# Left halo copies of the last chunk issued one feature block ahead on GpSimd

## The chip, the cores and the metric

One core of one Trainium2 chip. The metric is the device time of one execution in microseconds (us); the span that the profile shows is some 3.8 to 4.3 us shorter.

## The reference

A conformer block on x of 2 x 4000 x 512: feed-forward, attention, convolution module, feed-forward. The part concerned is the convolution module:

```python
h = a * sigmoid(b)                                # a, b: the two halves of layernorm(x2) @ w_pw1
hp = pad(h, one row of zeros before and after each sequence)
dc = sum(hp[:, i:i+T, :] * dw[i] for i in range(3))
dc = (dc - mean(dc)) / sqrt(var(dc) + 1e-5)       # per feature, over all 8000 tokens
x3 = x2 + silu(dc) @ w_pw2
```

## The kernel before

Tokens go in 16 chunks of 508 (444 for the last of each sequence), features in four blocks (jj or cc = 0 to 3). Of a chunk's gated values G, each block has one more column on either side, the halo, copied from the neighbour chunk or set to zero. Most of the convolution runs beside attention. For the last chunk (`last` = 15), and for parts of the two before it (`tail` = 14, and 13), it cannot, and stands in the open between attention and the second feed-forward. The mean and variance of a feature need all chunks, so this stretch ends in a dependence of everything on the last block.

The words used below: the taps are the three-tap convolution, here as matmuls on TensorE; the statistics and the aggregate (VectorE) give a feature's mean and variance; the power (GpSimd) and the shift (VectorE) turn them into a scale and an offset; a swish (ScalarE) is the silu of the normalised values. In code and views PE is TensorE, PEld its weight load, DVE VectorE, ACT ScalarE and POOL GpSimd.

The helper `S.op` makes an instruction wait for the last writer of each buffer that it reads or writes, and for the readers of those that it writes, unless an earlier wait of the same engine covers it already. `b_Gl` and `b_Gr` are the halo columns.

```python
def conv_a(self, t, jj):
    ps, b_ps = self.pw1(t, jj)                        # 4 matmuls on TensorE
    out = self.G[gs][:, jj, 1:1 + W]
    wr = [self.b_G[gs][jj], self.b_Gl[gs][jj], self.b_Gr[gs][jj]]
    ...                                               # tail: gates built elsewhere
    elif t == NCK - 1:
        self.halo_left(t, jj)
        self.S.op("DVE", ...scalar_tensor_tensor(     # the gate
            out=out, in0=ps[:, 0:W], scalar=2.0, in1=th, op0=ALU.mult, op1=ALU.mult),
            reads=[b_ps, self.b_th[k]], writes=wr)
    ...
    self.halo_right(t, jj)

def halo_left(self, t, jj):
    ...   # GpSimd: copy of one column from the chunk before, and for the last chunk
    ...   # of a sequence a memset of the right edge column

def conv_scale(self, cc):
    S.op("DVE", ...bn_aggr(...))                      # aggregate
    S.op("POOL", ...tensor_tensor(..., op=ALU.pow))   # power: 1/sqrt(var)

# the main loop over the blocks (cuts marked)
for jj in range(DC):
    self.conv_b(last, jj)                             # 4 matmuls, sigmoid on ACT
    if jj == DC - 1:
        self.act(self.nr1, self.onef, AF.Silu, ...)   # brings the table load here
    copy_away()                                       # ACT: PSUM banks of earlier taps to SBUF
    self.conv_a(last, jj)
    if jj > 1:
        self.conv_shift(jj - 2)                       # DVE: -mean/sqrt(var), reads the power
    if jj:
        finish(jj - 1)                                # taps on TensorE, statistics on DVE, conv_scale
    else:
        ...
self.swish(0, 0); self.swish(0, 1)                    # ACT
copy_away()
...
def between():
    self.conv_shift(DC - 2)
    self.swish(0, 2)
finish(DC - 1, between)                               # between its two statistics
self.conv_shift(DC - 1)
self.swish(0, 3)
copy_away()
```

## Time and profile before

| what | value |
|---|---|
| median, three runs (all that the prediction had) | 2045.01 us (2044.95 to 2045.12) |
| the profiled execution | 2043.9 us, span 2040.1 us |
| TensorE busy | 2029.2 us, 99% |
| two waits of the gate for the halo | 1.86 us in all |
| ACT idle before the last swish of chunk 0 | 0.68 us |

Read it so: TensorE carries nearly the whole span, so only the few places where the chain leaves it are worth anything. The kernel's lines are L1100 (gate), L1206 (statistics), L1213 (aggregate), L1215 (power), L1220 (shift), L1185 and L1188 (left halo and edge memset), L1195 (right halo). All matmuls have line L506 and all ACT instructions L556, those of a helper; "keys" on ACT are the bank copies, "work<-keys" the swishes. The changed kernel's lines are one or two less.

One measure is used below for every kernel. The chain of each trace has a run of 40 matmuls after attention and one of 20 at the second feed-forward. The time from the start of the one to the start of the other is called **the stretch**.

```profile
1516.88 8.74 PE s L506 x40
...
1551.66 4.32 PE s L506 x20
```

In the kernel before it is 1551.66 - 1516.88 = 34.78 us.

### The profile page before, as it was taken

How to read it: one execution, taken by the hardware profiler on the slowest of the kernel's cores; microseconds unless marked ns; L12 is line 12 of the kernel's file. 1: busy time of each engine (PE TensorE's matmuls, PEld its weight loads, DVE VectorE, ACT ScalarE, POOL GpSimd, SP SyncE). 2: the span in 40 equal slices, each digit the busy share in tenths (PEclk: the TensorE clock that was granted, in tenths of full speed). 3: DMA queues.
4: the chain of work that ended last, by engine and by line, in shares of the span. 5: the costliest groups of instructions: out<-in, count | busy, mean ns of one | idle time of the engine just before them, and what ended most of it. 6: DMA issues, size and time to landing. Idle time of an engine off the chain costs nothing.

```text
span 2040.1 us, 24550 instructions
## 1 busy us (share of the span) xinstructions
PE 2029.2 (99%) x9665; PEld 1029.8 (50%) x9667; DVE 1081.1 (53%) x2187; ACT 746.9 (37%) x1280; POOL 107.7 (5%) x235
## 2 busy tenths in 40 slices
PE   9999999999999999999999999999999999999998
PEld 5555555554444444445444444444455555555555
DVE  4234443334556667666766676667674444434433
ACT  3433333333333333333333333333345443443433
POOL 1000000000000000000000000000011000000000
PEclk9999999999999999999999999999999999999999
DMA  8222245320101111114421111111143111111111
GB/s 185 52 62 62 53 100 126 96 70 8 27 16 26 25 33 26 25 25 95 108 57 23 26 28 33 24 26 26 44 135 93 32 31 42 32 31 42 28 35 38
DMA packets 253122, 104.43 MB, mean 51 GB/s; under 512 B 193412, under 2 KB 252487, under 8 KB 252999
## 3 DMA queue, kind: packets, MB, share of 16 engines
q1 hardware_dynamic: 252751, 102.61, 20.9%
q8 instruction: 78, 1.28, 0.3%
q14 instruction: 45, 0.37, 0.1%
q10 hardware_dynamic: 248, 0.18, 0.0%
HBM read 33.77 MB, written 23.34 MB: 28 GB/s over the span
## 4 chain that ended last, share of the span: by engine, by line
PE 98%; DVE 1%; ACT 0%; DMA 0%; SPq 0%; POOL 0%; issue 0%; DVEq 0%; ACTq 0%
PE s L506 56%; PE y L506 42%; ACT work L556 0%; DVE wff L1206 0%; DMA wff<-in_w_ff_a_dram 0%; SPq L568 0%; POOL work L1215 0%; DVE work L553 0%; DVE wff L1100 0%; PE y L534 0%; ACT keys L556 0%; DVE work L1213 0%; SPq L560 0%; DVE work L869 0%; DVE work L952 0%
## 5 line engine op out<-in xcount | busy, mean ns | idle before, releaser
L556 ACT ACTIVATE work<-s 128x508 bf16<-128x508 f32 (+3 forms) x1060 | 622.7, 588 | 1211.8 <-PE s L506 1208.2
L506 PE MATMUL s<-work,wff 128*128 128x508 bf16 (+5 forms) x2624 | 628.3, 371 | 1.5 <-DVE work L553 0.8
L506 PE MATMUL s<-work,keys 128*128 128x508 bf16 (+1 forms) x2048 | 516.7, 374 | 0.1
L506 PE MATMUL y<-work,keys 128*128 128x508 bf16 (+2 forms) x2048 | 504.2, 373 | 0.4 <-DVE work L553 0.4
L506 PE MATMUL y<-wff,work 128*127 128x512 bf16 (+1 forms) x2000 | 501.4, 378 | 0.0
L952 DVE TENSOR_TENSOR work<-work 128x508 f32<-128x508 f32 (+2 forms) x496 | 334.6, 675 | 282.9 <-ACT work L556 281.8
L506 PEld LDWEIGHTS s<-work,wff 128*128 128x128 bf16 x2624 | 252.3, 98 | 278.0 <-issue 5.0
L506 PEld LDWEIGHTS y<-wff,work 128*127 128x127 bf16 x2000 | 274.4, 137 | 170.8
L506 PEld LDWEIGHTS s<-work,keys 128*128 128x128 bf16 x2048 | 199.4, 98 | 231.9 <-issue 0.6
L506 PEld LDWEIGHTS y<-work,keys 128*128 128x128 bf16 (+1 forms) x2048 | 193.5, 97 | 234.0 <-issue 6.2
L755 DVE SCALAR_TENSOR_TENSOR xt<-y,xt 127x512 bf16<-127x512 f32 x125 | 77.8, 684 | 364.9 <-PE y L506 364.9
L618 DVE BATCH_NORM_STATS2 work<-xt 127x6 f32<-127x512 bf16 x311 | 195.5, 678 | 4.8 <-DMA xt<-in_x_dram 4.7
L506 PE MATMUL s<-work 128*127 128x512 bf16 (+3 forms) x776 | 196.2, 377 | 1.6 <-DVE work L1324 1.2
L625 POOL TENSOR_TENSOR work<-work 127x4 f32<-127x4 f32 (+1 forms) x76 | 76.5, 1007 | 1130.4 <-DVE work L623 1130.4
L506 PEld LDWEIGHTS s<-work 128*127 128x127 bf16 (+1 forms) x776 | 94.7, 124 | 75.7 <-issue 2.7
L638 DVE TENSOR_SCALAR work<-xt,work 127x512 bf16<-127x512 bf16 x306 | 110.4, 407 | 27.0 <-POOL work L625 23.2
L755 DVE SCALAR_TENSOR_TENSOR xt<-s,xt 127x512 bf16<-127x512 f32 x55 | 38.0, 692 | 148.6 <-PE s L506 148.6
L755 DVE SCALAR_TENSOR_TENSOR xt<-s,work,xt 127x512 bf16<-127x512 f32 x64 | 48.0, 750 | 30.8 <-PE s L506 30.2
L1104 DVE SCALAR_TENSOR_TENSOR wff<-wff,s 128x508 bf16<-128x508 f32 (+1 forms) x57 | 38.7, 679 | 41.4 <-PE s L506 41.2
L556 ACT ACTIVATE wff<-s 128x508 f32<-128x508 f32 (+1 forms) x67 | 39.5, 591 | 54.6 <-PE s L506 54.6
L556 ACT ACTIVATE work<-keys,work 128x508 bf16<-128x508 bf16 (+1 forms) x68 | 52.3, 775 | 0.8 <-DVE work L1220 0.7
L1185 POOL COPY wff<-wff 128x1 bf16<-128x1 bf16 x56 | 10.4, 187 | 637.8 <-DVE wff L1104 635.0
(92 smaller groups left out, 415.7 us busy)
## 6 DMA issues: line engine op xcount, KB each, us to landing
keys<-keysd SPq DMA_DIRECT2D x62, 128.0 KB, 2.3
keysd<-work SPq DMA_DIRECT2D x14, 448.0 KB, 3.2
out_dram<-work SPq DMA_DIRECT2D x14, 448.0 KB, 3.2
dcvd<-wff SPq DMA_DIRECT2D x48, 127.0 KB, 1.8
keys<-dcvd SPq DMA_DIRECT2D x12, 508.0 KB, 5.4
xt<-in_x_dram SPq DMA_DIRECT2D x13, 448.0 KB, 4.7
wff<-in_w_ff_a_dram SPq DMA_DIRECT2D x16, 256.0 KB, 5.0
work<-work SPq DMA_TRANSPOSE x208, 2.5
```

Of the source, the lines that this page charges most:

```text
L506: self.S.op("PE", lambda e: e.matmul(out, lhsT, rhs, start=start, stop=stop, **kw), reads=reads, writes=[bank], inc=stop if inc is None el ...
L556: return self.S.op("ACT", lambda e: e.activation(out, in_, func, **kw), reads=reads, writes=writes)
L618: self.S.op("DVE", lambda e: e.bn_stats(self.st[sl][:, ti, 0:6], x), reads=[b_x], writes=[self.b_st[sl][ti]])
L625: S.op("POOL", lambda e: e.tensor_tensor(out=self.rs[sl][:, 0:n], in0=self.mv[sl][:, 0:n, 1], in1=self.neghalf[0:TILE, 0:n], op=ALU.pow), ...
L638: self.S.op("DVE", lambda e: e.tensor_scalar(out, x, self.mv[sl][:, ti, 0:1], self.rs[sl][:, ti:ti + 1], ALU.subtract, ALU.mult), reads=[b ...
L755: self.S.op("DVE", lambda e: e.scalar_tensor_tensor(out=self.XT[g][rows], in0=ps[rows], scalar=scalar, in1=self.XT[g][rows], op0=ALU.mult, ...
L952: S.op("DVE", lambda e, p=p, n=n, acc=acc: e.tensor_tensor(out=acc, in0=acc, in1=self.P[p][0:n, 0:W], op=ALU.add), reads=[self.b_P[p], sel ...
L1104: self.S.op("DVE", lambda e: e.scalar_tensor_tensor(out=out, in0=th, scalar=1.0, in1=ps[:, 0:W], op0=ALU.add, op1=ALU.mult), reads=[b_ps, ...
L1185: S.op("POOL", lambda e: e.tensor_copy(self.G[gs][:, jj, 0:1], self.G[gp][:, jj, CHUNK:CHUNK + 1]), reads=[self.b_G[gp][jj]], writes=[self ...
```

## The change

Its intent: the gate of a block should not wait for the batch norm power of a block two before it, only because the power stands ahead of the halo in GpSimd's queue. The left halo needs the chunk before alone, so it can be issued a block earlier.

```diff
@@ conv_a
         elif t == NCK - 1:
-            self.halo_left(t, jj)
             self.S.op("DVE", ...)
@@ main loop
+        self.halo_left(last, 0)
         for jj in range(DC):
             self.conv_b(last, jj)
             ...
             self.conv_a(last, jj)
             if jj > 1:
                 self.conv_shift(jj - 2)
+            if 0 < jj < DC - 1:
+                self.halo_left(last, jj + 1)
             if jj:
                 finish(jj - 1)
             else:
+                self.halo_left(last, 1)
                 f, copy = self.depthwise(tail - 1, DC - 1)
```

## The prediction

> **What bounds the kernel now.** I read the busy times, then the chain that ended last, then the same chain and the engine timelines in the one short stretch that the change touches.
>
> ```profile
> PE 2029.2 (99%) x9665; PEld 1029.8 (50%) x9667; DVE 1081.1 (53%) x2187; ACT 746.9 (37%) x1280; POOL 107.7 (5%) x235
> PE 98%; DVE 1%; ACT 0%; DMA 0%; SPq 0%; POOL 0%; issue 0%; DVEq 0%; ACTq 0%
> ```
>
> TensorE (PE) is busy 99% of the 2040.1 us span and carries 98% of the chain. The other engines together have about 2% of the chain. The change adds, drops and shrinks no instruction: it reorders eight tiny GpSimd (POOL) ones. So it can only move the time where the chain is off PE. The granted clock is 1.000, so there is nothing to win there.
>
> The change acts in the hand-over from attention to the second feed-forward, at 1524 to 1552 us, where the last chunk's four feature blocks (jj = 0 to 3) pass through the gate, the depthwise taps and the batch norm. The chain's pieces there:
>
> ```profile
> 1534.19 0.23 DVE work L1213
> 1534.42 0.07 issue
> 1534.49 0.55 POOL work L1215
> 1535.04 0.14 POOL wff L1185
> 1535.18 0.04 POOL wff L1188
> ...
> 1535.34 0.62 DVE wff L1100
> ...
> 1537.66 0.55 POOL work L1215
> 1538.21 0.14 POOL wff L1185
> 1538.35 0.04 POOL wff L1188
> ...
> 1538.51 0.32 DVE wff L1100
> ```
>
> L1213 is the batch norm aggregate, L1215 its power on GpSimd, L1185 and L1188 the left halo copy and the right edge memset of the next block, L1100 the gate multiply on VectorE (DVE) that writes the same G tile. The gate multiply is declared to write the halo column too, so it waits for the copy and memset; these stand behind the power in GpSimd's queue; the power waits for the aggregate. So the gate of block 2 waits for the norm of block 0, and that of block 3 for block 1: two detours. The waits of this stretch price them:
>
> ```profile
> DVE wff L1100 <- POOL wff L1188: 1.9, 2, 0.9
> ```
>
> Two waits of 0.93 us each. But the chain is not all of it: what follows in the queues decides how much is given back.
>
> ```profile
> 1535.89 1.66 PE L506 MATMUL s<-work,wff 128*128 128x444 bf16 x8
> 1539.38 1.38 PE L506 MATMUL y<-wff 128*128 128x444 bf16 x6 [0.19 <-ACT keys L556]
> 1544.36 1.08 PE L506 MATMUL s<-work 128*127 128x512 bf16 x4 [0.41 <-ACT work L556]
> ```
>
> PE runs without a gap from 1529.83 to about 1539.0; it never stands for the two DVE waits themselves (the table by stretches gives PE 3.10 of 3.10 us and 3.17 of 3.17 in the two block periods). The first gap after them ends on an ACT copy that empties a PSUM bank. The second ends on the last swish of chunk 0, and there the lateness of DVE comes due:
>
> ```profile
> 1537.40 1.28 ACT L556 ACT_TABLE_LOAD   x1
> 1543.50 0.81 ACT L556 ACTIVATE work<-keys,work 128x508 bf16<-128x508 bf16 x1 [0.68 <-DVE work L1220]
> ```
>
> ACT works without a pause from 1537.40, stands idle once for 0.68 us until the last shift (L1220), and is then full again (7.26 of 7.26 us in 1544.40 to 1551.66), through the copies, four swishes of chunk 1 and two layer norm tiles. After 1551.66 PE is again continuous. So **the 0.68 us of ACT idle is what the change can win**, not the 1.86 us of DVE idle.
>
> **What the Trainium skill says.**
> - "Perfetto Trace Analysis", section Tensor Engine Instruction: ACT, DVE and GPSIMD are strict FIFO. The trace agrees: the copy at 1534.99 starts 0.50 us after the power at 1534.49, though its data had been ready since 1525.99.
> - "GPSIMD Engine Reference", section 2.1 Instruction dispatch: completion gates what waits on the semaphore and does not hold back the next Pool instruction. The trace agrees: copies of 0.19 us start 0.12 us apart (1528.61, 1528.72, 1528.84). So the two moved instructions take about 0.23 us of GpSimd per block wherever they stand, not their summed durations.
> - "ScalarE: Activation LUTs", section What ACT_TABLE_LOAD costs: about 1283 ns, plus a drain of about 1380 ns. The trace agrees on the first (1.28 us) and shows no drain: the next ACT instruction starts at 1538.70, 1.30 us after the load started. I use 1.30.
>
> **The change part by part.**
>
> *Blocks 0 and 1: nothing.* Their halo copies move in the source, but GpSimd's order stays as it was: block 0's copy still follows the right halo of the chunk before, block 1's still follows the right halo of block 0. Gates at 1530.83 and 1532.24 unmoved.
>
> *Blocks 2 and 3, GpSimd.* Copy and memset now follow the right halo of the block before (1532.92, and the one after gate 2) and stand before the power. They are done at about 1533.3 for block 2, 1.2 us before that power's aggregate is there. The power itself is not delayed: GpSimd idled 1.38 and 1.45 us before it. Cost 0.
>
> *Gate of block 2.* Without the halo wait it waits for PE only. Gate 1, which did so, started at 1532.24, 0.10 us after its matmuls' modelled end (1530.48 + 1.66 = 1532.14). For block 2: 1533.19 + 1.66 + 0.10 = 1534.95, was 1535.34: 0.39 earlier. DVE is free since 1534.41.
>
> *Gate of block 3.* 1535.89 + 1.66 + 0.10 = 1537.65, was 1538.51: **0.86 earlier**. DVE is free: gate 2 at 1534.95, then 0.54 to the shift, 0.06 to the two statistics of 1.35, aggregate of 0.25, done by 1537.1 or so. PE's pace sets this, not DVE's; of 1.86 us of waits about 0.86 survives here.
>
> *Statistics of block 2.* Gate 3 at 1537.65, shift at 1538.19, statistics to 1539.6, aggregate from 1539.64 (was 1540.50).
>
> *Statistics of block 3.* Here the first give-back: the depthwise matmuls of block 3 cannot start before 1539.38, because their bank is emptied by an ACT copy that stands behind the table load (1537.40 + 1.30 + about 0.1, copy 1538.81 to 1539.3). That doesn't move, as the ACT queue before it hangs on PE. Their first half ends at about 1540.15, the second at 1540.76. So the first statistics go at 1540.2 (was 1540.66) and the second at 1540.86 (was 1541.59): **0.73 earlier**. From there 1.91 us to the last swish, as before (statistics, aggregate, power, shift: 1541.59 to 1543.50): 1542.77.
>
> *ACT.* The swish before it starts at 1542.00, and swishes follow each other about 0.7 us apart (four in 2.90), so ACT is free at about 1542.7. The last swish goes at 1542.77, 0.73 earlier; the idle of 0.68 shrinks to almost nothing. Its third neighbour, PE: the last four matmuls of chunk 0's second pointwise product follow at 1543.7 instead of 1544.36, some 0.62 to 0.66 earlier (PE is busy with the third group of four, loaded at 1542.87, until then).
>
> *After that.* ACT's full stretch moves by about 0.7, DVE's layer norm stretch from 1544.83 by about 0.62, and both meet in the transposes before 1551.66. The smaller shift holds: **0.65 us**, as a middle. The weights for the second feed-forward are loading (DMA share 1.00 and 1.09), but the last are issued at 1543.07 with 7.0 us to landing, and first used at 1555.82; a shift of 0.65 leaves a margin of several us for the first ones.
>
> *Added.* The shifts of blocks 0 and 1 now need a wait on the power of their own (the gate's wait covered it before), already fulfilled: hundredths of a us, in DVE time with slack.
>
> Sum: 2045.01 - 0.65 = **2044.36 us**, 0.03%.
>
> **The rivals.**
> 1. *The full waits come off:* 2 x 0.93 = 1.86 us, 2043.15. For: the chain names these very pieces. Against: PE has no gap in the two block periods, and its 2.70 us per block (1533.19 to 1535.89) is longer than what remains of DVE's 3.17 (3.17 - 0.93 = 2.24). Only the part beyond PE's pace can be won.
> 2. *The bank copies hold everything:* ACT's table load is the true bound, and the last swish has another wait; 2045.0. For: the first PE gap ends on that copy. Against: ACT shows a real idle of 0.68 us before the last swish, and its releaser is the shift on DVE.
> 3. *The gain is hidden by the weights:* the stretch after 1538.5 has a saturated DMA, and PE would then wait for a weight block in the second feed-forward; 2044.7 to 2045.0. For: DMA share 1.09. Against: no DMA wait stands in the chain here now.
> 4. *Slower:* the power delayed behind a halo that waits. The left halos wait for depthwise matmuls of the chunk before last that ended by 1530.5, so I see nothing for it.
>
> **Range and chances.** The main road is worth 0.6 to 0.7; rivals 2 and 3 together have perhaps one chance in six and pull up to 2045.0; rival 1 in part (a further 0.3 from ACT) one in ten. The three runs before differ by 0.17 us. So 2043.8 to 2045.0. Two per cent is 41 us, beyond anything a 28 us stretch can give: within 2% at 0.98.
>
> **What would show it.** Right: in the changed trace GpSimd has copy, memset and then the power twice; the two waits of L1100 on L1188 are gone; gate 3 starts about 0.86 earlier relative to its matmuls; PE's gap before the depthwise matmuls on the ACT copy stays at about 0.19; ACT's idle before the last swish falls from 0.68 to under 0.15; PE's gap of 0.41 before the last four matmuls shrinks to near 0. Wrong: gate 3 early but the last swish not (rival 2); the swish early but a new PE wait on a weight load after 1551 us (rival 3); the block period falling clearly below 2.70 us (rival 1).

## The result and the profile after

| | median us | lowest to highest | runs |
|---|---|---|---|
| before | 2045.07 | 2044.95 to 2045.14 | 4 |
| changed | 2043.54 | 2042.86 to 2044.69 | 4 |

The ratio is 0.9993, 95% interval 0.9976 to 1.001: within 2%, and 1.53 us between the medians, where 0.65 was predicted. The measured median lies below the predicted range (2043.8 to 2045.0).

The stretch in the chain of the changed kernel:

```profile
1517.07 8.74 PE s L506 x40
...
1551.13 4.32 PE s L506 x20
```

It is 34.06 us, 0.72 less than before. Here are the pieces between (cuts marked), which before led four times through the power on GpSimd:

```profile
1536.24 0.77 PE s L506 x4
...
1537.03 0.54 ACT wff L556
...
1537.59 1.28 ACT L556
...
1539.09 0.91 ACT keys L556 x2
1540.00 1.39 ACT work L556 x2
1541.39 0.91 ACT keys L556 x2
1542.30 1.47 ACT work L556 x2
1543.77 0.91 ACT keys L556 x2
1544.68 4.12 ACT work L556 x6
```

From 1530 us on no GpSimd and no DVE piece is left: TensorE hands over to ACT at the gate function of block 3 (1537.03), and from there the view gives everything to ACT: the table load, the copies and the swishes. The order on GpSimd (its timeline; columns: start, duration, engine, line, operation) is the intended one:

```profile
1533.23 0.19 POOL L1184 COPY wff<-wff 128x1 bf16<-128x1 bf16 x1
1533.34 0.10 POOL L1187 MEMSET wff<- 128x1 bf16 x1
1534.67 0.55 POOL L1214 TENSOR_TENSOR work<-work 128x1 f32<-128x1 f32 x1 [1.23 <-DVE work L1212]
```

The gates now wait for their matmuls alone (DVE's timeline; in brackets the idle time before and what ended it):

```profile
1535.13 0.62 DVE L1099 SCALAR_TENSOR_TENSOR wff<-s,wff 128x444 bf16<-128x444 f32 x1 [0.54 <-PE s L506]
...
1537.84 0.62 DVE L1099 SCALAR_TENSOR_TENSOR wff<-s,wff 128x444 bf16<-128x444 f32 x1 [0.47 <-PE s L506]
```

The last two swishes of chunk 0 (ACT's timeline) and the last 16 matmuls of its pointwise product (TensorE's) now follow each other, where before 0.68 and 0.41 us of idle time stood ahead of the last ones:

```profile
1542.18 1.59 ACT L556 ACTIVATE work<-keys,work 128x508 bf16<-128x508 bf16 x2
```

```profile
1541.22 3.77 PE L506 MATMUL s<-work 128*127 128x512 bf16 x16
```

The two views hide a close finish. Asked for the last swish and the last shift alone, ACT's and DVE's timelines give:

```profile
1542.96 0.81 ACT L556 ACTIVATE work<-keys,work 128x508 bf16<-128x508 bf16 x1
```

```profile
1542.77 0.16 DVE L1219 SCALAR_TENSOR_TENSOR work<-work 128x1 f32<-128x1 f32 x1 [0.73 <-POOL work L1214]
```

The last swish starts 0.19 us after the shift, as it did before (1543.30 and 1543.50). In an unbroken pair the second swish follows 0.70 us after the first, so ACT would have been ready at 1542.88. The shift on DVE still comes last, by 0.08 us, and ACT's queue stands right behind it.

So the stretch gave 0.72 us, nearly the predicted 0.65. Where are the other 0.8 us of the medians? The two profiled spans differ by 0.9 (2040.1 and 2039.2), and this can be laid out whole. The chain reaches its 40 matmuls at 1516.88 before and at 1517.07 after: the changed kernel was 0.19 us **behind** before the change had touched anything. The stretch takes 0.72 off. From the 20 matmuls to the issue of the last store on ACT's queue both take the same (1551.66 to 2036.71 is 485.05; 1551.13 to 2036.17 is 485.04). From that issue to the end of the span it is 3.4 us before and 3.0 after. The sum: +0.19 - 0.72 - 0.01 - 0.33 = -0.87. Beside the change the two traces differ in their opening and in the landing of the last store, and nowhere else to a few hundredths of a us.

### The profile page after: what moved, and what is told of

Its sections match the earlier page's. It is cut to its first block, busy times and chain, and to the rows that moved or that the text cites. A ratio compares the mean times of both kernels' runs of the same rounds, so it can differ in the third digit from the quotient of the medians.

```text
span 2039.2 us, 24554 instructions
## 1 busy us (share of the span) xinstructions
PE 2029.2 (100%) x9667; PEld 1030.0 (51%) x9667; DVE 1080.7 (53%) x2187; ACT 746.0 (37%) x1280; POOL 107.6 (5%) x235
## 4 chain that ended last, share of the span: by engine, by line
PE 98%; ACT 1%; DVE 0%; DMA 0%; SPq 0%; issue 0%; ACTq 0%
PE s L506 56%; PE y L506 42%; ACT work L556 0%; DMA wff<-in_w_ff_a_dram 0%; ACT keys L556 0%; SPq L568 0%; DVE work L553 0%; PE y L534 0%; ACT L556 0%; SPq L560 0%; DVE work L869 0%; DVE work L952 0%; DVE wff L1205 0%; DVE wff L1092 0%; ACT wff L556 0%
```

## The experiments

**Theory A**: the change is worth 0.72 us, and the rest is spread from run to run, at the beginning and the end. **Theory B**: the change wins some 0.8 us more somewhere. Within A, further runs ask what the mechanism is: what the halves of the change do, what a longer power costs before and after, and what bounds the stretch now.

The stretch of each kernel, from its chain (start of the 40, start of the 20):

| kernel | 40 | 20 | stretch | against before |
|---|---|---|---|---|
| before | 1516.88 | 1551.66 | 34.78 | |
| changed | 1517.07 | 1551.13 | 34.06 | -0.72 |
| changed, again | 1516.59 | 1550.66 | 34.07 | -0.71 |
| changed, third time | 1517.42 | 1551.49 | 34.07 | -0.71 |
| before, unchanged | 1517.24 | 1552.02 | 34.78 | 0.00 |
| block 3 alone | 1516.80 | 1550.86 | 34.06 | -0.72 |
| block 2 alone | 1516.38 | 1550.77 | 34.39 | -0.39 |
| before, long warm-up | 1558.09 | 1592.87 | 34.78 | 0.00 |
| changed, long warm-up | 1558.68 | 1592.75 | 34.07 | -0.71 |
| before, powers doubled | 1516.51 | 1552.56 | 36.05 | +1.27 |
| changed, powers doubled | 1516.65 | 1551.24 | 34.59 | -0.19 |
| changed, copies before table load | 1516.66 | 1550.65 | 33.99 | -0.79 |
| changed, early table load | 1516.66 | 1550.59 | 33.93 | -0.85 |
| the same, shift after statistics | 1517.27 | 1550.98 | 33.71 | -1.07 |

The same kernel repeats its stretch to 0.01 us, on at least three chips, while the times of one kernel spread over 2 us.

### 1. The changed kernel again

No edit.

> The changed kernel once more, beside the kernel before on one chip. Theory A (the change is worth only the 0.72 us that the two traces show between TensorE's block at 1530 us and the second feed-forward at 1551 us, and the rest of the 1.5 us of the medians is spread from execution to execution): the ratio of fast runs is 0.9996 to 0.9997 (0.6 to 0.9 us), with single runs of one kernel spread by 1 us or more, and the same stretch in a new trace 0.72 us shorter to within 0.05. Theory B (the change also wins 0.8 us somewhere outside the stretch): the ratio stays near 0.9993 (1.5 us), and the new trace has the second shortening again, at a place that can be named.

Measured: median 2043.58 (2042.98 to 2043.87, 5 runs), before 2044.14 (2043.13 to 2044.6, 9 runs); ratio 0.9999 (0.9985 to 1.0012). The stretch is 34.07. The kernel before has now runs as low as 2043.13, nearly 2 us below its first four. The stretch is as A has it. The ratio is nearer to 1 than either theory said, with an interval that holds both: times alone cannot decide this.

### 2. The kernel before against itself

No edit.

> The kernel before, unchanged, submitted as if it were a change: what the comparison shows when there is nothing to show. Theory A: difference of medians up to about 0.5 us either way, single runs spread over 1 us or more, and no difference at all in the trace between 30 us and 2000 us after the start. Theory B: runs within 0.2 us, as the first four runs of the kernel before were, so that 1.5 us would be well outside the spread.

Measured: median 2044.31 (2043.29 to 2045.13, 5 runs), ratio 1.0002 (0.9988 to 1.0015); stretch 34.78, as before. Nothing was changed, the medians differ by 0.17 us, and the runs spread over 1.8 us. That is A; the tight first four runs were no measure of the spread. The two traces of this kernel, matched instruction by instruction between 30 and 2000 us, keep one distance of 0.36 us to within 0.03 us: no difference along the way, as A expected.

### 3. Block 3's half alone

```diff
         elif t == NCK - 1:
-            self.halo_left(t, jj)
+            if jj < DC - 1:
+                self.halo_left(t, jj)
@@ main loop, ahead of finish(jj - 1)
+            if jj == DC - 2:
+                self.halo_left(last, jj + 1)
```

> Only block 3's left halo goes ahead of a batch norm power; block 2's stays behind one as before. Theory A (TensorE paces the gates, and only the lateness of the last one reaches the last swish on ACT): gate 2 starts as before, gate 3 as in the changed kernel (0.47 us idle on DVE ends on TensorE), the last swish as in the changed kernel: 0.70 to 0.72 us of the stretch, as much as both. Rival R1 (each removed wait is worth its half): 0.36 us.

```profile
1535.26 0.62 DVE L1101 SCALAR_TENSOR_TENSOR wff<-s,wff 128x444 bf16<-128x444 f32 x1 [0.93 <-POOL wff L1189]
...
1537.57 0.62 DVE L1101 SCALAR_TENSOR_TENSOR wff<-s,wff 128x444 bf16<-128x444 f32 x1
```

This is DVE's timeline of that kernel. Gate 2 still waits 0.93 us for the halo. Gate 3 starts where the changed kernel has it (1537.84 there, less the 0.27 us by which this trace is ahead at the 40 matmuls), though without the 0.47 us of idle time that was expected before it: DVE, late from gate 2, is free only just in time. The stretch is 34.06: **the whole gain, with one of two waits left in place**. Median 2042.94 (5 runs), ratio 0.9996 (0.9982 to 1.0009). As A expected; R1 (0.36 us) falls.

### 4. Block 2's half alone

```diff
         elif t == NCK - 1:
-            self.halo_left(t, jj)
+            if jj != DC - 2:
+                self.halo_left(t, jj)
@@ main loop, ahead of finish(jj - 1)
+            if jj == DC - 3:
+                self.halo_left(last, jj + 1)
```

> Only block 2's left halo goes ahead; block 3's stays behind the power of block 1. Theory A: gate 2 starts 0.39 us earlier, so the aggregate, the power and block 3's halo are earlier by as much; gate 3 starts about 0.4 earlier, at about 0.45 later than in the changed kernel; its statistics still just meet the depthwise matmuls that wait for the bank copy on ACT, so the last swish is 0.6 to 0.72 us earlier: nearly the whole gain again, and the two halves do not add. Rival R1: 0.36 us.

```profile
1537.61 0.62 DVE L1101 SCALAR_TENSOR_TENSOR wff<-s,wff 128x444 bf16<-128x444 f32 x1 [0.93 <-PE y L506]
...
1540.59 0.16 DVE L1221 SCALAR_TENSOR_TENSOR work<-work 128x1 f32<-128x1 f32 x1 [0.25 <-POOL work L1216]
```

The stretch is 34.39, 0.39 less. I expected 0.6 to 0.72: a miss, and close to R1's figure, though R1 was refuted by the run before. Gate 3 still starts 0.93 us after DVE was free (the view names TensorE as what ended it; the memset of its halo at 1537.38 is there in GpSimd's timeline). What the expectation overlooked is in the second line: the shift of block 2 stands between the two statistics of block 3, and here waits 0.25 us for block 2's power. So there was no slack behind gate 3 that could take up part of its lateness; the 0.39 by which gate 2 is earlier runs through unreduced. The halves give 0.72 and 0.39, together 0.72: they do not add, as block 3's half alone takes the lateness away. Median 2043.15 (5 runs), ratio 0.9998.

### 5. The power doubled, in the kernel before

```diff
-        S.op("POOL", ...pow..., writes=[self.b_rsc[cc]])
+        for _ in range(2 if cc < 2 else 1):
+            S.op("POOL", ...pow..., writes=[self.b_rsc[cc]])
```

> The kernel before with the batch norm power of blocks 0 and 1 done twice in a row on GpSimd (same input, same result): the halos of blocks 2 and 3 come some 0.55 to 0.6 us later each. Theory A (in the kernel before, DVE and GpSimd in a ring carry the chain through both blocks, as block 2's half of the change alone gave 0.39 of the 0.72 us): the waits of the gates grow from 0.93 to about 1.5 us each and the stretch from TensorE's block at 1530 us to the second feed-forward grows by 1.1 to 1.2 us. Rival R2 (the table load on ACT and TensorE's pace bound the stretch, the power is mostly hidden): under 0.3 us.

```profile
DVE wff L1100 <- POOL wff L1188: 3.1, 2, 1.6
```

In the waits of 1532 to 1544.5 us, the gates' wait for the halo has grown from 1.9 us to 3.1 in all, and the stretch by 1.27 us, 0.63 to each power. In the kernel before, what is added between the aggregate and the halo comes through in full, at both powers. A holds (its 1.1 to 1.2 was slightly low), R2 falls.

### 6. The power doubled, in the changed kernel

The same edit.

> The same doubled powers in the changed kernel, where they stand behind the halos. Theory A: gates stay on TensorE; the doubled power of block 1 delays its shift and the statistics after it by about 0.3 us, which the 0.27 us of DVE idle before block 3's statistics takes up: the stretch as in the changed kernel, within 0.05 us. Rival R2: as much longer as in the kernel before with the same dose.

```profile
1535.54 0.17 DVE L1220 SCALAR_TENSOR_TENSOR work<-work 128x1 f32<-128x1 f32 x1 [0.20 <-POOL work L1215]
...
1538.62 0.16 DVE L1220 SCALAR_TENSOR_TENSOR work<-work 128x1 f32<-128x1 f32 x1 [0.58 <-POOL work L1215]
```

The stretch is 34.59, **0.53 longer** than the changed kernel's: my expectation of nothing was wrong, and R2, which expected 1.27, too. The gates are free, but the next reader of the power in DVE's queue, the shift, now waits (0.20 and 0.58 us), and the statistics wait behind it. The ring of DVE and GpSimd (shift, statistics and aggregate on DVE, power on GpSimd, and back to the next shift) is still there, only shorter: from shift to shift it takes 1538.62 - 1535.54 = 3.08 us with the doubled power, so by estimate 3.08 - 0.63 = 2.45 with the single one. (The traces of experiments 7 and 8 have it directly: there, too, the shift of block 2 waits for its power, and comes 2.43 us after the shift before it, 1537.97 to 1540.40.) TensorE needs 2.71 for a block (1533.37 to 1536.08 in the changed kernel). The change has thus made the ring some 0.26 us per block shorter than TensorE's pace, and no more. Before, through the gate, it took 3.17.

### 7. The bank copies ahead of the table load

Applied to the changed kernel.

```diff
+            copy_away()
             if jj == DC - 1:
                 self.act(self.nr1, self.onef, AF.Silu, ...)
-            copy_away()
```

> The changed kernel, with the two bank copies of block 1 on ACT ahead of the table load instead of behind it. Theory A (ACT itself is full in the changed kernel from the table load to the layer norm, and that is what now sets the stretch): TensorE's gap of 0.18 us before block 3's depthwise matmuls goes, its statistics are 0.35 to 0.45 us earlier, the last swish is not: the stretch within 0.1 us of the changed kernel's. Rival R3 (the bank copy sets the last swish through the statistics): 0.35 to 0.45 us shorter.

The matmuls of block 3's taps now follow without the wait for the bank copy (TensorE's timeline, 1538.82 in this kernel with no idle time noted), and the stretch is 0.07 us shorter. A expected under 0.1, R3 0.35 to 0.45. But the cause is not quite A's. Counted from the 40 matmuls, block 3's first statistics are 0.34 us earlier than in the changed kernel, the second and the last shift only 0.14, because block 2's shift now waits 0.19 us for its power between them. Of these 0.14 the last swish takes up 0.05: its pair is now unbroken (1541.80, 1.50 us for two), so ACT's queue holds it. In the changed kernel the shift holds the last swish; ACT's queue stands 0.05 to 0.08 us behind it, and block 2's power is the next thing on DVE.

### 8. The table load in ACT's idle time

Applied to the changed kernel: the table load goes ahead of block 3's gate function, where ACT had 1.25 us of idle time. The gate function becomes a tanh.

```diff
-        if t < NCK - 2 or t == NCK - 2 and jj < self.KEEP:
+        if t < NCK - 2 or t == NCK - 2 and jj < self.KEEP or t == NCK - 1 and jj == DC - 1:
             self.act(...AF.Tanh..., scale=0.5)
@@ conv_a
-        elif t == NCK - 1:
+        elif t == NCK - 1 and jj < DC - 1:
@@ main loop
-            self.conv_b(last, jj)
             if jj == DC - 1:
                 self.act(self.nr1, self.onef, AF.Silu, ...)
+            self.conv_b(last, jj)
```

> The changed kernel, with the table load for the swish moved into ACT's idle time before the gate function of block 3, which then is a tanh with (1 + tanh) in the gate, as the other chunks have it (2 sigmoid(x) = 1 + tanh(x/2)). Theory A (ACT sets the stretch in the changed kernel): ACT has 1.3 us less to do behind block 3's matmuls, so the chain passes back to the depthwise matmuls, statistics, power and shift of block 3: the last swish and the stretch 0.35 to 0.5 us earlier than in the changed kernel, 1.1 to 1.2 less than before the change; two table loads in all in this stretch, none in the chain. Rival R4 (the tanh isn't in the loaded set): a further table load of 1.28 us shows up and the stretch gets longer.

```profile
1542.42 0.81 ACT L556 ACTIVATE work<-keys,work 128x508 bf16<-128x508 bf16 x1 [1.01 <-DVE work L1219]
```

No further table load appears, so R4 falls. ACT now stands idle 1.01 us before the last swish: DVE alone holds it. But the stretch is only 0.13 us shorter than the changed kernel's, where I expected 0.35 to 0.5. DVE's timeline shows the shift of block 2 waiting 0.19 us for its power between the two statistics of block 3, as in experiment 7, so the last shift is again 0.13 us earlier and no more; with ACT out of the way all of that arrives. The ring of experiment 6 is the next bound.

### 9. The shift behind the statistics

On top of experiment 8:

```diff
-        def between():
-            self.conv_shift(DC - 2)
-            self.swish(0, 2)
-        finish(DC - 1, between)
+        finish(DC - 1)
+        self.conv_shift(DC - 2)
+        self.swish(0, 2)
         self.conv_shift(DC - 1)
```

> The kernel with the early table load, with the shift of block 2 moved behind block 3's two statistics, so that VectorE no longer waits for block 2's power between them. Theory A (there the shift's wait of 0.19 us and the order of the queue hold block 3's second statistics, as the 0.58 us wait of the shift did in the changed kernel with doubled powers): that wait goes, the statistics end 0.2 to 0.3 us earlier, and the stretch is 0.2 to 0.3 us shorter than with the early table load alone, 1.05 to 1.15 us shorter than before the change. Rival R5 (TensorE or ACT holds the last swish there): no gain, within 0.05 us.

```profile
1540.20 1.40 DVE L1205 BATCH_NORM_STATS2 wff<-y 128x6 f32<-128x444 f32 x2
```

The two statistics of block 3 now follow each other without a wait, and the stretch is 33.71: 0.22 less than with the early table load alone, 1.07 less than before the change. As A expected; R5 falls. Median 2042.99 (2041.99 to 2043.74, 5 runs), before 2044.25 (9 runs); ratio 0.9992 (0.9979 to 1.0006). By its stretch it is the fastest version, ahead of both kernels; by its times it could not be told from them.

### 10. A long warm-up, before and changed

```diff
-        self.warm(14)
+        self.warm(214)
```

> The kernel before with 200 more of the idle matmuls that open the program (about 43 us more), so that the first loads have all landed when TensorE begins its work. Theory A (the spread of one kernel from run to run comes from the landing of the first loads, 8.6 to 9.5 us in the traces so far, and of the last store, 5.8 to 6.9 us): the first part is the same in this trace and in that of its partner to within 0.05 us, and the spread of the runs shrinks to that of the last store, about 1 us. Theory C (the spread lies along the whole program, in the granted clock): as wide as ever, over 1.5 us.

> The changed kernel with the same 200 matmuls more. Theory A: its median is 0.4 to 1.0 us below its partner's, the stretch around the change 0.72 us shorter in the trace, everything between the opening and the last store equal to within 0.03 us. Theory B (the change wins 1.5 us): 1.3 us or more below.

The medians are 2085.94 (2085.12 to 2086.79) and 2085.82 (2085.37 to 2086.21), 0.12 us apart: outside what A said, and further from B; with means 0.33 us apart and a standard error of 0.33, these ten runs cannot decide on 0.72. The stretches are 34.78 and 34.07. The expectation that the opening would be the same in both traces failed. Before (first fence) and changed (second), from TensorE's timeline:

```profile
1.18 47.35 PE L506 MATMUL s<-work 128*128 128x508 bf16 x214 [1.18 <-DVE work L1324]
```

```profile
1.18 47.94 PE L506 MATMUL s<-work 128*128 128x508 bf16 x214 [1.18 <-DVE work L1323]
```

The same 214 matmuls, on the same data, took 0.59 us longer in the one. This has nothing to do with loads. In the one trace the first 7 steps from matmul to matmul take 0.34 to 0.43 us, in the other the first 10 take 0.30 to 0.43, and the later ones 0.21; the trace's clock record has the step to the full clock 3.9 us after the start in the one, 5.1 in the other. The 1.2 us of half clock between cost 0.6. The Trainium skill says this: "TensorE: Matmul & The Clock Gate", Part 1, has a free-running activity window, so that the same kernel shows a different number of cold matmuls from run to run. With the long warm-up this chance stands in every time, where the short one hid part of it behind the first loads (block 3 alone has its clock step 2.6 us later than the kernel before, and reaches the 40 matmuls 0.08 us earlier). The runs spread over 1.7 and 0.8 us, the one as theory C said and the other as theory A. The traces speak against C: from the warm-up to block 2's gate the two keep their distance of 0.59 us to within 0.03.

### 11. The changed kernel a third time

No edit.

> The changed kernel a third time, for the mean over many runs. In the traces so far the clock of TensorE comes up to full 3.8 to 6.8 us after the start of the program and the last store lands 5.8 to 6.9 us after the last matmuls, both by chance; everything between repeats to 0.03 us. Theory A: the mean of all runs of the changed kernel so far and of these is 0.72 us below the mean of all runs of the kernel before, within 0.5 us; the stretch in this trace is again 35.90 to 35.92 us between the same two weight loads (36.62 before). Theory B (1.5 us): the means differ by 1.2 or more.

Median 2043.27 (2042.9 to 2044.22, 5 runs), before 2044.37 (9 runs); ratio 0.9996 (0.9982 to 1.0009); stretch 34.07. (The expectation's 35.90 and 36.62 lie between two weight loads that it does not name; the difference, 0.71, is the same.) Over all runs: **the changed kernel's 14 have a mean of 2043.56 us (standard deviation 0.54), the 36 of the kernel before 2044.35 (0.60)**. The difference is 0.78, with a standard error of 0.18 (root of 0.54 x 0.54 / 14 + 0.60 x 0.60 / 36). That agrees with the 0.72 of the traces; 1.5 us lies four standard errors away. Theory B falls, with the caution that the runs come from several rounds and chips. The first round, which raised the question, does not make the result: without it the means are 0.73 apart.

## Why the prediction was right or wrong

**The mechanism was right, and nearly to the number.** All of the following are the prediction's figures with the 0.19 us added by which the changed trace was behind at the start (written 0.19; both traces are rounded to 0.01).

| step | predicted | measured |
|---|---|---|
| gate 2 | 1534.95 + 0.19 = 1535.14 | 1535.13 |
| gate 3 | 1537.65 + 0.19 = 1537.84 | 1537.84 |
| block 3's first statistics | 1540.2 + 0.19 | 1540.34 |
| block 3's second statistics | 1540.86 + 0.19 = 1541.05 | 1541.06 |
| last swish | 1542.77 + 0.19 = 1542.96 | 1542.96 |
| TensorE's gap on the bank copy | stays at 0.19 | 0.18 |
| TensorE's gap of 0.41 | near 0 | gone |
| ACT idle before the last swish | under 0.15 | 0.09 (1.59 for two swishes, 1.50 for an unbroken pair) |
| the stretch | 0.65 less | 0.72 less |

The one term of this sum that was mis-sized is "The smaller shift holds": 0.65, from 0.62 on DVE and 0.7 on ACT. With 0.19 added to the times before, DVE's layer norm came 0.64 us earlier (1544.83 to 1544.38), ACT's bank copies behind the last swish (1544.21 to 1543.68) and its layer norm tiles (1547.91 to 1547.38) 0.72, and the second feed-forward 0.72: the larger one, ACT's, held. Experiment 7 agrees: its DVE layer norm stands where the changed kernel's does, to 0.01 us, and its stretch is still 0.07 shorter.

**Rival 1** (the full 1.86 us) is refuted by every trace: gate 3 could win 0.86 because TensorE's pace stood there. **Rival 2** fell with the stretch. **Rival 3** fell: the 485 us from the second feed-forward to the last store are the same to 0.01 us. **Rival 4** fell: the power of block 0 starts at 1534.67, where it did (1534.49 + 0.19).

**What failed is the step "2045.01 - 0.65", and the range drawn from "the three runs before differ by 0.17 us".** Those three runs, and the fourth, lie at the upper end of what this kernel does: 2045.06 in the mean, against 2044.35 over 36 runs that reach from 2043.13 to 2045.27. The median of the changed kernel's first four runs, 2043.54, is usual for it (mean of 14: 2043.56). So of the 1.53 us between the first medians, 0.72 are the change and some 0.7 the base (2045.06 - 2044.35). From a base of 2044.35 the same working gives 2043.70, and the measured median is 0.16 below that. The page of before held a warning that the prediction did not use: the profiled execution took 2043.9 us, 1.1 less than the three runs, and was the same kernel.

What makes the spread is shown in part. The opening: the chain reaches the 40 matmuls between 1516.38 and 1517.42 us in the traces with the short warm-up, by when the clock comes up and when the first weights land. The end: from the issue of the last store on ACT's queue to the end of the span it is 2.9 us in one trace (2035.91 to 2038.8, block 3 alone) and 4.0 in another (2035.63 to 2039.6, early table load). Each is 1.0 to 1.1 us wide, and between them next to nothing moves. **What stays open** is why the first four runs of the kernel before lie so close together at the upper end; no trace of those runs was taken.

**One remark of the prediction was too easy:** the extra wait of the shifts, "in DVE time with slack". There is slack, but 0.26 us per block and no more (experiment 6). Likewise the 2.24 us that it left to DVE per block (3.17 - 0.93) drop the wait for the power altogether; experiments 7 and 8 have 2.43, still under TensorE's 2.70, so the conclusion stood. Three of its readings are off by a little, without effect: 1525.99 is the start of the gate that writes the copied column (it ends at 1526.68), the taps that rival 4 names end at 1530.65, and TensorE's run without a gap at 1539.20.

## What to carry to other kernels

Taking a wait off an in-order queue hands it to the next reader of the same result: find out how far behind that one is, by doubling the late operation before and after the change. Two waits in a row on a paced pipeline need not be worth their sum: here they were 1.86 us and gave 0.72, what was left of them at the end, and half of the change brought all of it. Where a chain view gives a stretch to one engine, look for the other that finishes within a tenth of a us of it. Where an effect is under a microsecond, compare equal points in two traces, and take the base of a forecast from many runs, not from three that happen to agree.

## What the Trainium skill lacked or had wrong

- "ScalarE: Activation LUTs", What ACT_TABLE_LOAD costs: it adds a drain of about 1380 ns to the 1283 ns of the load. No trace here shows it: the next ACT instruction starts 1.30 us after the load (1537.40 to 1538.70 before; 1535.39 to 1536.69 with the early table load).
- "TensorE: Matmul & The Clock Gate", Part 1: the chance in the number of cold matmuls is there, and agrees (7 and 10 slow steps in the two traces with the long warm-up). What it lacks is what this does to a comparison of two kernels: 0.59 us between two runs with 214 matmuls at the start, near the size of the change studied.
- No page that I read has the spread of the last store's landing: 2.9 to 4.0 us from its issue to the end of the span.
- No page that I read has the cost of a dependent GpSimd instruction behind another: two powers with a wait between them start 0.63 us apart (1534.12 and 1534.75), where a copy that does not depend on the power starts 0.50 behind it (1534.49 and 1534.99).
